# Feed-forward blocks of 512 tokens, one per batch, with the last 64 tokens of each batch set aside in DRAM for a ninth block

## The chip, the cores and the metric

The kernel runs on one core of one Trainium2 chip. The metric is the device time of one execution in microseconds. TensorE is called PE below (its weight loads PEld), VectorE DVE, ScalarE ACT, GpSimd POOL; SP is the engine that issues nearly all DMAs, from one queue in order.

## The reference

Eight batches of 576 tokens, model width 512. Each batch goes through attention over pooled keys and values, a two-dimensional Fourier transform whose real part is added, a normalization, and a feed-forward layer of width 2048, which holds most of the arithmetic:

```python
k_p = k.reshape(B, H, Sp, pool, D).mean(axis=3)          # pool = 8, Sp = 72
attn = softmax(scale * q @ k_p^T)                        # 8 heads of 64
x = (attn @ v_p).transpose(0, 2, 1, 3).reshape(B, S, 512)
mixed = np.real(fft(fft(x, axis=1), axis=2))
u = x + mixed
un = (u - mean(u)) / sqrt(var(u) + 1e-6)
out = u + np.maximum(un @ w_ch1, 0.0) @ w_ch2            # 512 -> 2048 -> 512
```

## The kernel before

**Two kinds of work share PE.** `fe(b)` is the front end of batch b: everything up to the normalized tokens. `ffn(...)` is the feed-forward layer on a block of token columns. Both are generators: each `yield` ends a stage, and the loop at the bottom of `tile_kernel` emits one stage of `ffn`, then the stages of front ends that are due (`advance`). A scheduler then places every instruction on its engine's queue, a fixed order in which the engine runs them; it can pull a front end's instructions ahead of or behind feed-forward matmuls.

**Front end.** With PE's tiles in the order in which they run: scores `psS` (L345) for four pairs of heads, transposes `psT`, `psV`, `psR`, values `psX`, then the transform over channels `psA` and `psB` (L547, L575), the transform over tokens `psQ` and `psP` (L592), the mean `psM` (L638 to L643) and the variance `psVar`. From `psQ` on the front end writes the batch's slot. The steps between the last of them: DVE adds `psP` to `X` (L607, L608), DVE sums two tiles into `s` (L617), ACT and DVE split `s` into two parts (L619, L620), POOL forms the four tiles of `U` (L624, L625), PE takes the mean (`psM`), DVE subtracts it (L644), ACT casts the result to `unh` (L632), DVE and POOL form the rest `unl` (L633). `unh` and `unl` are what the feed-forward matmuls read. The reciprocal deviation `rb` comes after that and is needed only when a block ends.

**The slots.** `U`, `unh`, `unl` and `rb` are rings of 1152 columns, two slots of 576: batch b lies in slot (b+1) mod 2. A front end may write its slot (stage "U") when the feed-forward layer has read the batch two before it; `free[b]` is the position at which that is so.

**Feed-forward.** A block takes 16 steps f, one for each 128 of the width 2048. A step has 12 matmuls into `g` (L731: `w1h` with `unh`, `w1h` with `unl`, `w1low` with `unh`, each over four channel tiles), ACT's relu to `hh` (L735), DVE's remainder `hl` (L736), and 12 matmuls into the four accumulators `acc` (L715). A step's second half is issued after the next step's first half. At the end of a block DVE multiplies each accumulator by `rb` (L745), adds it to `U` (L746), and SP writes `out` (L748). The blocks before: batch 0 in two halves of 288 columns, each in two passes over 8 steps; batches 1 to 6 in three rings of 1152 columns, each in three blocks of 384 that pass over the border between two batches; batch 7 in two blocks of 288. That is 208 steps, 64 of them with 288 columns and 144 with 384.

**Weights.** They come in 64-bit floats; 34 pieces are converted by ACT and DVE, split by ACT and POOL into a high part that stays and a low part that goes to DRAM (L205). Each step loads its two low parts of 256 KB back (L214), one step or more ahead, into a ring of 7 buffers that the conversion uses too. 11 pieces are converted before the first block (`AHEAD`), the others at positions that `PACE` and `LEAD` set.

Of the kernel before, what the change touches and what calls it, by code (L numbers as in the profile page):

```python
# [21 lines left out]
HS = S // 2  # L22
# [56 lines left out]
def raw(ap):  # L79
# [4 lines left out]
def tile_kernel(ctx: ExitStack, tc: tile.TileContext, qt, kt, vm, vr, w1, w2, cad, cbd, mkd, out):  # L84
# [76 lines left out]
    def load_w(n):  # L161
        if n >= len(pieces):
            return
        i, f, c, w, place = pieces[n]
        src = (w1, w2)[i][:, f, c * P:(c + w) * P]
        if not wide:
            st = wk.tile([P, DM], F32, tag="w", bufs=7, name="wraw")[:, 0:w * P]
            nc.sync.dma_start(st, src)
            staged[n] = st
            return  # L170
        if place is not None:
            st = wk.tile([P, 2 * DM], I32, tag=f"tail{place}", name="wst")
        else:
            st = wk.tile([P, DM], I32, tag="w", bufs=7, name="wraw")
        nc.sync.dma_start(st, src.bitcast(I32))
        staged[n] = st.rearrange("p (c m w) -> p c m w", m=P, w=2)

    def prep_w(n):
        if n >= len(pieces):
            return  # L180
        i, f, c, w, _ = pieces[n]
        cl = slice(c * P, (c + w) * P)
        if wide:
            st = staged.pop(n)
# [62 lines left out]
    def fe(b):  # L247
# [82 lines left out]
        def scores(gi, i):  # L330
# [371 lines left out]

    at = [0]

    def ffn(ro, nb, to, f0, f1):
        cl = slice(ro, ro + nb)
        acc = [pp.tile([P, 512], F32, tag=f"acc{e}", name=f"acc{to}_{f0}_{e}")[:, 0:nb] for e in range(4)]

        def gemm2(f, hh, hl, wh, wl):
            order = [(x, e) for x in range(3) for e in range(4)]  # L710
            if f == f1 - 1:
                order = [(x, e) for e in range(4) for x in range(3)]
            for x, e in order:
                w, h = ((wh, hh), (wl, hh), (wh, hl))[x]
                nc.tensor.matmul(acc[e], lhsT=w[:, e], rhs=h, start=(f == f0 and x == 0), stop=(f == f1 - 1 and x == 2))  # L715

        prev = None
        for f in range(f0, f1):
            step = at[0]
            at[0] += 1  # L720
            for m in range(2):
# [5 lines left out]
            ps = pp.tile([P, 512], F32, tag="g1", bufs=2, name=f"g1_{to}_{f}")[:, 0:nb]  # L727
            n = 0
            for w, x in ((ah, unh), (ah, unl), (al, unh)):
                for c, ti in enumerate((E0, O0, E1, O1)):  # L730
                    nc.tensor.matmul(ps, lhsT=w[:, c], rhs=x[:, ti, cl], start=(n == 0), stop=(n == 11))  # L731
# [7 lines left out]
                gemm2(f - 1, *prev)  # L739
                yield  # L740
            prev = (hh, hl, bh, bl)
        gemm2(f1 - 1, *prev)
        for e in range(4):
            u = U[:, e, cl]
            nc.vector.tensor_tensor(out=acc[e], in0=acc[e], in1=rb[:, cl], op=ALU.mult)  # L745
            nc.vector.tensor_tensor(out=u, in0=u, in1=acc[e], op=ALU.add)  # L746
            if f1 == NFC and e % 2:
                nc.sync.dma_start(out[:, e - 1:e + 1, to:to + nb], U[:, e - 1:e + 1, cl])  # L748
# [39 lines left out]
    def advance(pos):  # L790
        for b in sorted(run):
# [6 lines left out]
            while r[1] < upto:  # L798
# [133 lines left out]
```

## Time and profile before

| | before |
|---|---|
| median of 3 runs | 1094.45 us (1093.58 to 1095.3) |
| profiled execution: span | 1094.2 us |
| PE busy, share of the span | 1050.1 us, 96% |
| DVE, ACT, POOL busy | 611.6, 416.0, 247.3 us |
| DMA moved, mean rate | 175.80 MB, 161 GB/s |
| loads of low weights | 2 x 208 of 256 KB |
| PE instructions | 6606 |

The profiled execution is the span of 1094.2 us, 0.25 us from the median. In a timeline row stand the start, the busy time, the engine, the line, the operation, the tiles and their shape, the number of instructions merged into the row, and in brackets how long the engine had been idle before it and who released it. In a row of waits stand the total, the number and the longest. A row of groups has the busy time and the mean of one instruction.

### The profile page before, as it was taken

The numbers are of one execution on the slowest core, as the hardware profiler recorded it, in microseconds if no ns is written. First come the engines' busy times: TensorE is split into PE (matmuls) and PEld (weight loads), VectorE is DVE, ScalarE is ACT, GpSimd is POOL, SyncE is SP. The second block draws the span as 40 slices with busy tenths as digits, with TensorE's granted clock in tenths as the row PEclk, the third lists the DMA queues.
The fourth block names the chain that finished last, engine by engine and source line by source line (L and its number), as shares of the span: only waits on it lengthen the run. The fifth ranks groups of instructions, "written<-read, shape, count | busy, mean of one in ns | idle before, by whom it ended". The sixth has DMA issues, their size and how long they took to land.

```text
span 1094.2 us, 17702 instructions
## 1 busy us (share of the span) xinstructions
PE 1050.1 (96%) x6606; PEld 1017.7 (93%) x6606; DVE 611.6 (56%) x1237; ACT 416.0 (38%) x1102; POOL 247.3 (23%) x249
## 2 busy tenths in 40 slices
PE   8848898999999999999999999999999999999997
PEld 7637887999999999999999999999999999999997
DVE  7686878856376455756377455756467434522222
ACT  6767764443143331443233341443324322311110
POOL 4463356212230032201240121400322101200000
PEclk9968999999999999999999999999999999999999
DMA  7867977565345454445444444445534334346563
GB/s 242 274 204 254 318 250 227 178 199 170 119 122 161 121 162 135 127 140 166 131 120 148 142 151 130 133 125 156 158 108 155 98 98 124 117 128 189 165 186 99
DMA packets 91878, 175.80 MB, mean 161 GB/s; under 512 B 10128, under 2 KB 17296, under 8 KB 91536
## 3 DMA queue, kind: packets, MB, share of 16 engines
q1 hardware_dynamic: 91504, 172.01, 50.7%
q0 software_dynamic: 288, 2.66, 0.7%
q8 instruction: 52, 0.85, 0.3%
q14 instruction: 34, 0.28, 0.1%
HBM read 156.81 MB, written 17.83 MB: 160 GB/s over the span
## 4 chain that ended last, share of the span: by engine, by line
PE 84%; DVE 6%; DMA 4%; ACT 3%; issue 1%; POOL 1%; SPq 0%; DVEq 0%; POOLq 0%; ACTq 0%
PE acc L715 35%; PE g L731 35%; PE psX L432 3%; PE psS L345 3%; PE psA L547 2%; PE psP L592 2%; DMA wst<-in_w 1%; DMA w1low<-w1l 1%; PE psB L575 1%; PE psT L385 1%; DVE wd L199 1%; PE psQ L592 1%; DVE wd L198 1%; DMA k<-in_kt 1%; PE psR L408 1%
## 5 line engine op out<-in xcount | busy, mean ns | idle before, releaser
L735 ACT ACTIVATE hh<-g 128x384 fp32r<-128x384 f32 (+1 forms) x208 | 96.3, 464 | 309.6 <-PE g L731 289.8
L736 DVE SCALAR_TENSOR_TENSOR hl<-g,hh 128x384 fp32r<-128x384 f32 (+1 forms) x208 | 108.6, 522 | 185.0 <-ACT hh L735 183.2
L715 PE MATMUL acc<-hh,w2h 128*128 128x384 f32 (+1 forms) x832 | 190.9, 329 | 0.1
L715 PE MATMUL acc<-hh,w2low 128*128 128x384 f32 (+1 forms) x832 | 187.6, 328 | 1.2 <-DMA w2low<-w2l 1.2
L715 PE MATMUL acc<-hl,w2h 128*128 128x384 f32 (+1 forms) x832 | 182.6, 328 | 0.7 <-DVE hl L736 0.7
L731 PE MATMUL g<-unh,w1low 128*128 128x384 f32 (+1 forms) x832 | 178.7, 329 | 4.5 <-DMA w1low<-w1l 4.4
L731 PE MATMUL g<-unl,w1h 128*128 128x384 f32 (+1 forms) x832 | 178.1, 329 | 0.9 <-DVE unl L633 0.9
L731 PE MATMUL g<-unh,w1h 128*128 128x384 f32 (+1 forms) x832 | 175.4, 327 | 0.1
L731 PEld LDWEIGHTS g<-unh,w1low 128*128 128x128 f32 x832 | 140.8, 190 | 6.2 <-DMA w1low<-w1l 5.8
L715 PEld LDWEIGHTS acc<-hh,w2low 128*128 128x128 f32 x832 | 144.4, 189 | 2.0 <-DMA w2low<-w2l 1.4
L715 PEld LDWEIGHTS acc<-hh,w2h 128*128 128x128 f32 x832 | 143.2, 189 | 2.8 <-ACT rt L372 0.8
L715 PEld LDWEIGHTS acc<-hl,w2h 128*128 128x128 f32 x832 | 141.5, 190 | 1.5 <-DVE hl L736 0.9
L731 PEld LDWEIGHTS g<-unl,w1h 128*128 128x128 f32 x832 | 140.4, 190 | 2.1 <-DVE unl L633 1.3
L731 PEld LDWEIGHTS g<-unh,w1h 128*128 128x128 f32 x832 | 140.4, 190 | 1.5 <-issue 0.8
L364 POOL TENSOR_TENSOR t<-t,sm 128x720 f32<-128x720 f32 x32 | 45.9, 1434 | 286.7 <-DVE sm L363 248.0
L280 POOL TENSOR_TENSOR k<-k 128x288 f32<-128x288 f32 (+1 forms) x56 | 41.0, 732 | 97.6 <-DMA k<-in_kt 84.3
L624 POOL TENSOR_TENSOR U<-X,U 128x576 f32<-128x576 f32 (+1 forms) x14 | 20.0, 1433 | 129.2 <-DVE X L608 129.2
L349 DVE TENSOR_REDUCE mx<-psS 128x6 f32<-128x432 f32 (+1 forms) x64 | 33.1, 526 | 19.6 <-PE psS L345 19.3
L345 PE MATMUL psS<-kpb,q 128*128 128x144 f32 x280 | 42.7, 286 | 1.3 <-ACT w2h L203 0.9
L345 PEld LDWEIGHTS psS<-kpb,q 128*128 128x128 f32 x280 | 39.4, 189 | 1.7 <-ACT w2h L203 1.1
L360 ACT ACTIVATE t<-t 128x720 f32<-128x720 f32 x30 | 24.1, 804 | 37.1 <-DVE t L358 36.8
L745 DVE TENSOR_TENSOR acc<-acc,rb 128x384 f32<-128x384 f32 (+1 forms) x60 | 29.0, 517 | 13.5 <-PE acc L715 13.5
(209 smaller groups left out, 1426.9 us busy)
## 6 DMA issues: line engine op xcount, KB each, us to landing
w1low<-w1l SPq DMA_DIRECT2D x208, 256.0 KB, 2.8
w2low<-w2l SPq DMA_DIRECT2D x208, 256.0 KB, 2.9
wst<-in_w SPq DMA_DIRECT2D x30, 512.0 KB, 4.7
q<-in_qt SPq DMA_DIRECT2D x28, 288.0 KB, 3.1
k<-in_kt SPq DMA_DIRECT2D x28, 288.0 KB, 2.9
v<-in_vm SPq DMA_DIRECT2D x28, 256.0 KB, 3.0
out<-U SPq DMA_DIRECT2D x18, 384.0 KB, 3.6
w1l<-wd SPq DMA_DIRECT2D x16, 256.0 KB, 5.1
```

What stands on the lines that cost most here:

```text
L280: nc.gpsimd.tensor_tensor(out=out if n == 1 else src[:, :, 0:n], in0=src[:, :, 0] if n == 1 else src[:, :, 0:n], in1=src[:, :, 1] if n == ...
L345: mm = nc.tensor.matmul(ps[:, c * W2J:(c + 1) * W2J], lhsT=q[:, r0:r0 + P], rhs=kpb[g % 2], start=True, stop=True)
L349: nc.vector.tensor_reduce(out=mx[:, c0:c0 + n], in_=pv, op=ALU.max, axis=AX.X, negate=(b, g) in SM)
L360: nc.scalar.activation(t, t, AF.Exp, scale=1.0 / 64.0)
L364: ins = nc.gpsimd.tensor_tensor(out=t, in0=t, in1=sm.unsqueeze(3).broadcast_to([P, 5, 2, J]), op=ALU.mult)
L432: last = nc.tensor.matmul(ps, lhsT=w, rhs=a, start=(i == 0), stop=(i == len(mm) - 1))
L592: nc.tensor.matmul(ps, lhsT=w, rhs=a, start=(i == 0), stop=(i == 6))
L715: nc.tensor.matmul(acc[e], lhsT=w[:, e], rhs=h, start=(f == f0 and x == 0), stop=(f == f1 - 1 and x == 2))
L731: nc.tensor.matmul(ps, lhsT=w[:, c], rhs=x[:, ti, cl], start=(n == 0), stop=(n == 11))
L735: nc.scalar.activation(hh, ps, AF.Relu)
L736: nc.vector.scalar_tensor_tensor(out=hl, in0=ps, scalar=0.0, in1=raw(hh), op0=ALU.max, op1=ALU.subtract)
L745: nc.vector.tensor_tensor(out=acc[e], in0=acc[e], in1=rb[:, cl], op=ALU.mult)
```

## The change

`blocks()` now gives nine blocks of 512 columns: the first 512 tokens of each batch, in the slot where the batch lies, then a ninth block that is read from slot 0's place. All 16 steps run over each block: 144 steps. The first step of all is done in two column ranges, 288 and 224.

New are `keep_rest(b)`, issued when the front end of batch b has ended, which writes the last 64 columns of `unh`, `unl`, `U` and `rb` to four DRAM tiles `rests` (three DMAs of 128 KB and one of 32 KB for each batch, in pieces of 256 bytes), and `load_rest`, which before the ninth block reads the 8 x 64 columns of all batches back (three DMAs of 1 MB and one of 256 KB). The free positions, the pace of the weight conversion and the order in which the output is put together follow. `hh` and `hl` have 512 columns, and the ring of weight buffers has 6 places.

Lines of the changed kernel are 2 on from L731 (L733), L735 (L737) and L745 (L747); L715 keeps its number, as do those of the front end.

```diff
-AHEAD, LEAD, PACE = 11, 12, 0.65
+NB = 512
+RM = S - NB
+AHEAD, LEAD, PACE = 11, 8, 1.0
 def blocks():
-    r = [(slot(0) + h * HS, HS, h * HS, f, f + 8) for f in (0, 8) for h in range(2)]
-    for m in range(3):
-        r += [(i * 384, 384, S + m * RING + i * 384, 0, NFC) for i in range(3)]
-    return r + [(slot(7) + h * HS, HS, 7 * S + h * HS, 0, NFC) for h in range(2)]
+    return [(slot(b % B), b * NB) for b in range(B + 1)]
...
+    rests = [dp.tile([P, n, B, RM], F32, name=f"rest{i}") for i, n in enumerate((4, 4, 4, 1))]
...
-        lows[i, n] = t = wk.tile([P, DM], F32R, tag="w", bufs=7, name=f"w{i + 1}low")
+        lows[i, n] = t = wk.tile([P, DM], F32R, tag="w", bufs=6, name=f"w{i + 1}low")
...
-    def ffn(ro, nb, to, f0, f1):
-        cl = slice(ro, ro + nb)
+    def ffn(ro, to):
+        cl = slice(ro, ro + NB)
...
-            for w, x in ((ah, unh), (ah, unl), (al, unh)):
-                for c, ti in enumerate((E0, O0, E1, O1)):
-                    nc.tensor.matmul(ps, lhsT=w[:, c], rhs=x[:, ti, cl], start=(n == 0), stop=(n == 11))
-                    n += 1
-            hh = wk.tile([P, 384], F32R, tag="hh", bufs=2, name="hh")[:, 0:nb]
-            hl = wk.tile([P, 384], F32R, tag="hl", bufs=2, name="hl")[:, 0:nb]
+            for c0, c1 in ((0, HS), (HS, NB)) if step == 0 else ((0, NB),):
+                n = 0
+                for w, x in ((ah, unh), (ah, unl), (al, unh)):
+                    for c, ti in enumerate((E0, O0, E1, O1)):
+                        nc.tensor.matmul(ps[:, c0:c1], lhsT=w[:, c], rhs=x[:, ti, ro + c0:ro + c1], start=(n == 0), stop=(n == 11))
+                        n += 1
+            hh = wk.tile([P, NB], F32R, tag="hh", bufs=2, name="hh")
+            hl = wk.tile([P, NB], F32R, tag="hl", bufs=2, name="hl")
...
+    def keep_rest(b):
+        cl = slice(slot(b) + NB, slot(b) + S)
+        for t, r in zip((raw(unh), raw(unl), U), rests):
+            nc.sync.dma_start(r[:, :, b], t[:, :, cl])
+        nc.sync.dma_start(rests[3][:, 0, b], rb[:, cl])
+
+    def load_rest(ro):
+        cl = slice(ro, ro + NB)
+        for t, r in zip((raw(unh), raw(unl), U), rests):
+            nc.sync.dma_start(t[:, :, cl], r.rearrange("p n b s -> p n (b s)"))
+        nc.sync.dma_start(rb[:, cl], rests[3].rearrange("p n b s -> p (n b s)"))
-    free = {1: 0, 2: 64, 3: 128, 4: 160, 5: 224, 6: 256, 7: 320}
+    free = {b: 2 * NFC * (b - 1) for b in range(1, B)}
...
-        return max(AHEAD + PACE * pos, pos - 16 + LEAD)
+        return max(AHEAD + PACE * pos, pos + LEAD)
...
-    for blk in blocks():
+    for n, blk in enumerate(blocks()):
+        if n == B:
+            load_rest(blk[0])
```

How the queues of two engines change at a block's end: first PE, where the front end of batch 7 passes `psP`'s last matmuls in the queue before. The names give the tile and a running number (`psP_2_10037` is the last of three `psP`, `g_3648` the `g` of the block that starts at token 3648).

```order
L731 MATMUL g_3648_3_10110<-unh,w1low 128x384 x4
L592 MATMUL psP_2_10037<-cb,A_9128 128x290 x3
L592 MATMUL psP_2_10037<-cb,A_9129 128x290 x3
L592 MATMUL psP_2_10037<-cb,AB_9130 128x290
L715 MATMUL acc_0_0_9939<-hh,w2h 128x384
L715 MATMUL acc_0_1_9940<-hh,w2h 128x384
L715 MATMUL acc_0_2_9941<-hh,w2h 128x384
L715 MATMUL acc_0_3_9942<-hh,w2h 128x384
```

In the queue before, `psP` stands between two feed-forward steps, and `psM` follows it 36 feed-forward matmuls later. Now PE's queue at the same place of batch 5's front end, from `psP`'s last tile on; `g_2560` is the first tile of batch 5's own block.

```order
L592 MATMUL psP_2_5755<-cb,A_5388 128x290 x3
L592 MATMUL psP_2_5755<-cb,A_5389 128x290 x3
L592 MATMUL psP_2_5755<-cb,AB_5390 128x290
L345 MATMUL psS_3_0_5813<-kpb_80,q_3_5798 128x144 x3
L345 MATMUL psS_3_3_5819<-kpb_80,q_3_5798 128x144 x2
L642 MATMUL psM_5843<-s,avg 128x288
L643 MATMUL psM_5843<-s,avg 128x288
L642 MATMUL psM_5847<-s,avg 128x288
L643 MATMUL psM_5847<-s,avg 128x288
L345 MATMUL psS_2_0_5921<-kpb_79,q_2_5880 128x144 x3
L345 MATMUL psS_2_3_5927<-kpb_79,q_2_5880 128x144 x2
L733 MATMUL g_2560_0_6732<-unh,w1h 128x512
```

No feed-forward matmul stands between `psP` and `psM`, nor between `psM` and the first `g` of the block that needs the result. Ahead of these rows stand `psB`, `psQ` and the first two `psP`, again without a feed-forward matmul, and ahead of those the last matmuls of the block before. From `psP` on, the same stands at all seven places where a batch follows another (without the scores `psS` at the last). Second, DVE's queue before, where the end of a block meets batch 7's `psB`:

```order
L530 TENSOR_TENSOR B_9180<-psB_0_9182,B_9180 128x256
L745 TENSOR_TENSOR acc_0_0_9397<-acc_0_0_9397,rb 128x384
L530 TENSOR_TENSOR B_9181<-psB_1_9212,B_9181 128x256
L745 TENSOR_TENSOR acc_0_1_9398<-acc_0_1_9398,rb 128x384
L746 TENSOR_TENSOR U<-U,acc_0_0_9397 128x384
```

The two large `psB` parts are taken before most of the block's eight closing operations. Now the same on DVE, at the end of batch 4's block:

```order
L747 TENSOR_TENSOR acc_3_5660<-acc_3_5660,rb 128x512
L748 TENSOR_TENSOR U<-U,acc_0_5657 128x512
L748 TENSOR_TENSOR U<-U,acc_1_5658 128x512
L530 TENSOR_TENSOR B_5440<-psB_0_5442,B_5440 128x256
L748 TENSOR_TENSOR U<-U,acc_2_5659 128x512
L530 TENSOR_TENSOR B_5441<-psB_1_5472,B_5441 128x256
L748 TENSOR_TENSOR U<-U,acc_3_5660 128x512
L535 TENSOR_TENSOR AB_5390<-psB_2_5481,AB_5390 32x256
L598 TENSOR_TENSOR U<-X,psQ_1_5682 128x288
```

Three of the four multiplications stand ahead of these rows: all parts of `psB`, which `psQ` waits for, now follow six to eight of the closing operations.

More of the change, by code (lines that the diff above doesn't have):

```diff
@@ L166, in load_w @@
         if not wide:
-            st = wk.tile([P, DM], F32, tag="w", bufs=7, name="wraw")[:, 0:w * P]
+            st = wk.tile([P, DM], F32, tag="w", bufs=6, name="wraw")[:, 0:w * P]
             nc.sync.dma_start(st, src)
@@ L173, in load_w @@
         else:
-            st = wk.tile([P, DM], I32, tag="w", bufs=7, name="wraw")
+            st = wk.tile([P, DM], I32, tag="w", bufs=6, name="wraw")
         nc.sync.dma_start(st, src.bitcast(I32))
@@ L186, in prep_w @@
             halves = st.bitcast(U16)
-            d0 = wk.tile([P, DM], I32, tag="w", bufs=7, name="wd")[:, 0:w * P]
+            d0 = wk.tile([P, DM], I32, tag="w", bufs=6, name="wd")[:, 0:w * P]
             di = d0.rearrange("p (c m) -> p c m", m=P)
@@ L211, in load_low @@
     def load_low(i, n):
-        lows[i, n] = t = wk.tile([P, DM], F32R, tag="w", bufs=7, name=f"w{i + 1}low")
+        lows[i, n] = t = wk.tile([P, DM], F32R, tag="w", bufs=6, name=f"w{i + 1}low")
         nc.sync.dma_start(raw(t), wls[i][:, steps[n]])
-    steps = [f for *_, f0, f1 in blocks() for f in range(f0, f1)]
+    steps = [f for _ in blocks() for f in range(NFC)]
     turn, behind = [0], {}
@@ L368, in scores @@
                 if b == 0 and gi:
-                    st["rt", gi] = wk.tile([P, DM], F32, tag="w", bufs=7, name="rt0")[:, 0:10 * REM].rearrange("p (c r) -> p c r", c=5)
+                    st["rt", gi] = wk.tile([P, DM], F32, tag="w", bufs=6, name="rt0")[:, 0:10 * REM].rearrange("p (c r) -> p c r", c=5)
                 else:
@@ L703, in tile_kernel @@
     at = [0]
-    def ffn(ro, nb, to, f0, f1):
-        cl = slice(ro, ro + nb)
-        acc = [pp.tile([P, 512], F32, tag=f"acc{e}", name=f"acc{to}_{f0}_{e}")[:, 0:nb] for e in range(4)]
+    def ffn(ro, to):
+        cl = slice(ro, ro + NB)
+        acc = [pp.tile([P, NB], F32, tag=f"acc{e}", name=f"acc{to}_{e}") for e in range(4)]
         def gemm2(f, hh, hl, wh, wl):
             order = [(x, e) for x in range(3) for e in range(4)]
-            if f == f1 - 1:
+            if f == NFC - 1:
                 order = [(x, e) for e in range(4) for x in range(3)]
@@ L714, in gemm2 @@
                 w, h = ((wh, hh), (wl, hh), (wh, hl))[x]
-                nc.tensor.matmul(acc[e], lhsT=w[:, e], rhs=h, start=(f == f0 and x == 0), stop=(f == f1 - 1 and x == 2))
+                nc.tensor.matmul(acc[e], lhsT=w[:, e], rhs=h, start=(f == 0 and x == 0), stop=(f == NFC - 1 and x == 2))
         prev = None
-        for f in range(f0, f1):
+        for f in range(NFC):
             step = at[0]
@@ L726, in ffn @@
             ah, al, bh, bl = [x.rearrange("p (c m) -> p c m", m=P) for x in (high(0, f), lows[0, step], high(1, f), lows[1, step])]
-            ps = pp.tile([P, 512], F32, tag="g1", bufs=2, name=f"g1_{to}_{f}")[:, 0:nb]
-            n = 0
-            for w, x in ((ah, unh), (ah, unl), (al, unh)):
-                for c, ti in enumerate((E0, O0, E1, O1)):
-                    nc.tensor.matmul(ps, lhsT=w[:, c], rhs=x[:, ti, cl], start=(n == 0), stop=(n == 11))
-                    n += 1
-            hh = wk.tile([P, 384], F32R, tag="hh", bufs=2, name="hh")[:, 0:nb]
-            hl = wk.tile([P, 384], F32R, tag="hl", bufs=2, name="hl")[:, 0:nb]
+            ps = pp.tile([P, NB], F32, tag="g1", bufs=2, name=f"g1_{to}_{f}")
+            for c0, c1 in ((0, HS), (HS, NB)) if step == 0 else ((0, NB),):
[6 more added lines that the diff above has]
+            hl = wk.tile([P, NB], F32R, tag="hl", bufs=2, name="hl")
             nc.scalar.activation(hh, ps, AF.Relu)
@@ L741, in ffn @@
             prev = (hh, hl, bh, bl)
-        gemm2(f1 - 1, *prev)
+        gemm2(NFC - 1, *prev)
         for e in range(4):
@@ L746, in ffn @@
             nc.vector.tensor_tensor(out=u, in0=u, in1=acc[e], op=ALU.add)
-            if f1 == NFC and e % 2:
-                nc.sync.dma_start(out[:, e - 1:e + 1, to:to + nb], U[:, e - 1:e + 1, cl])
+            if e % 2:
+                nc.sync.dma_start(out[:, e - 1:e + 1, to:to + NB], U[:, e - 1:e + 1, cl])
         yield
-    free = {1: 0, 2: 64, 3: 128, 4: 160, 5: 224, 6: 256, 7: 320}
+    def keep_rest(b):
[9 more added lines that the diff above has]
+    free = {b: 2 * NFC * (b - 1) for b in range(1, B)}
     npre = 20
@@ L777, in tile_kernel @@
                 pass
+            keep_rest(0)
         if n >= NEXT and n2 < 8:
@@ L780, in tile_kernel @@
             n2 += 1
+    keep_rest(1)
     while n2 < STEPS:
@@ L808, in advance @@
                     del run[b]
+                    keep_rest(b)
                     break
     def need(pos):
-        return max(AHEAD + PACE * pos, pos - 16 + LEAD)
+        return max(AHEAD + PACE * pos, pos + LEAD)
     pos = 0
-    for blk in blocks():
+    for n, blk in enumerate(blocks()):
+        if n == B:
+            load_rest(blk[0])
         for _ in ffn(*blk):
@@ L927 @@
     o = r.results[0]["out_0"]
-    o = o.transpose(2, 1, 0).reshape(B, S, DM)
+    o = o.transpose(2, 1, 0).reshape(B * S, DM)
+    o = np.concatenate([o[:B * NB].reshape(B, NB, DM), o[B * NB:].reshape(B, RM, DM)], 1)
     got = np.empty((B, S, DM), np.float32)
```

## The prediction

> **What bounds the kernel now.** I read the page first: the engines' busy time, and the span in 40 slices of 27.4 us.
>
> ```profile
> PE 1050.1 (96%) x6606; PEld 1017.7 (93%) x6606; DVE 611.6 (56%) x1237; ACT 416.0 (38%) x1102; POOL 247.3 (23%) x249
> PE   8848898999999999999999999999999999999997
> PEclk9968999999999999999999999999999999999999
> GB/s 242 274 204 254 318 250 227 178 199 170 119 122 161 121 162 135 127 140 166 131 120 148 142 151 130 133 125 156 158 108 155 98 98 124 117 128 189 165 186 99
> ```
>
> From the ninth slice on PE never rests, while DVE is at 56%. So PE's own work sets the time, and what counts is how much of it there is and whether PE must ever wait. The waits of PE from 60 us to the end come next.
>
> ```profile
> PE psT L385 <- POOL t L364: 7.3, 1, 7.3
> PE psM L638 <- DVE s L617: 6.0, 1, 6.0
> PE g L731 <- DMA w1low<-w1l: 4.4, 4, 1.9
> PE psVar L698 <- DVE X L695: 3.4, 1, 3.4
> PE psR L408 <- ACT ah L390: 1.7, 1, 1.7
> PE acc L715 <- DMA w2low<-w2l: 1.2, 1, 1.2
> ```
>
> The two largest, 13.3 us, lie before the first feed-forward matmul: there batch 0's front end has nothing to run beside it, and PE waits for its chain. No other front end costs PE such a wait, because feed-forward matmuls fill the gaps. Then the stretches with feed-forward matmuls alone (six steps of 384 columns, then 288), and the start and end of the feed-forward part in the timeline.
>
> ```profile
> core 0: us, PE busy (x) PEld busy (x) DVE busy (x) ACT busy (x) POOL busy (x), PEclk, DMA share, GB/s
> 60.00:90.00 30.00, 15.75 (x79) 14.26 (x80) 24.93 (x46) 20.70 (x62) 17.27 (x13) 0.66 0.64 206
> 956.63:981.84 25.21, 25.21 (x145) 25.21 (x145) 7.12 (x12) 4.32 (x8) 0.00 (x0) 1.00 0.43 125
> 1040.00:1085.00 45.00, 45.00 (x341) 45.00 (x340) 7.32 (x17) 5.78 (x15) 0.00 (x0) 1.00 0.53 159
> ```
> ```profile
> 76.94 2.03 PE L731 MATMUL g<-unh,w1h 128*128 128x288 f32 x7
> ...
> 1087.41 0.69 PE L715 MATMUL acc<-hl,w2h 128*128 128x288 f32 x4
> 1090.05 1.12 SPq L748 DMA_DIRECT2D out<-U  x2
> ```
>
> **Part 1, wider matmuls.** Six steps are 144 matmuls: 25.21 / 144 = 175.1 ns for 384 columns; 45.00 / 341 = 132.0 ns for 288. The difference is 0.449 ns a column, so 512 columns should take 175.1 + 128 x 0.449 = 232.5 ns. Before: 3456 x 175.1 + 1536 x 132.0 = 807.9 us. After: 144 x 24 = 3456 x 232.5 = 803.5 us. All of it lies on PE's path: **-4.4 us**. If 512 columns cost in proportion to 384 (233.5 ns), it is -1; I let it go to -8.
>
> **Part 2, the first block.** A new low weight is needed every 24 x 232.5 = 5.6 us instead of every 3.2, but all 16 pairs are now needed within 89 us, not 102. The waits for `w1low` and `w2low` above, 5.6 us together, shrink but need not vanish: **-4 us** (0 to -6). The waits for `psVar` and `psR` stay.
>
> **Part 3, the boundary.** This is the term that decides. PE's queue now holds a bare front end at each of seven places: from the block's last matmul through `psB`, `psQ`, `psP`, `psM` to the next block's first `g`. What that chain takes I read where batch 7's front end passes it, in the timeline of all engines.
>
> ```profile
> 930.04 0.29 PE L592 MATMUL psP<-cb,AB 98*128 98x290 f32 x1
> 930.17 0.86 PE L715 MATMUL acc<-hh,w2h 128*128 128x384 f32 x4
> 930.43 0.74 DVE L607 TENSOR_TENSOR X<-X,psP 128x574 f32<-128x574 f32 x1
> 931.28 0.76 DVE L617 TENSOR_TENSOR s<-X 128x576 f32<-128x576 f32 x1
> 933.41 1.82 POOL L625 TENSOR_TENSOR U<-X,U 128x576 f32<-128x576 f32 x1
> 937.27 0.43 PE L643 MATMUL psM<-s,avg 128*128 128x288 f32 x2
> 937.67 2.62 DVE L644 TENSOR_TENSOR X<-U,psM 128x1152 f32<-128x1152 f32 x2 [1.96 <-PE psM L643]
> 940.33 2.40 ACT L632 CAST unh<-X 128x576 fp32r<-128x576 f32 x4 [0.46 <-DVE X L644]
> 942.23 2.92 POOL L633 TENSOR_TENSOR unl<-X,unh 128x576 fp32r<-128x576 f32 x2 [7.00 <-ACT unh L632]
> ```
>
> Each waits for those above it. From `psP`'s end (930.17) to the end of the first cast (940.33 + 2.40 / 4 = 940.93) are 10.8 us. In it `psM` was held behind feed-forward matmuls: L644 needs POOL's `U`, ready at 935.23, and began at 937.67, 2.4 us late. So 8.4 us remain. In their place DVE has the next batch's scores to do, from these groups:
>
> ```profile
> L361 DVE TENSOR_REDUCE sm<-t 128x10 f32<-128x720 f32 x30 | 27.0, 899 | 15.3 <-ACT t L360 15.0
> L349 DVE TENSOR_REDUCE mx<-psS 128x6 f32<-128x432 f32 x32 | 19.3, 603 | 17.0 <-PE psS L345 16.8
> L358 DVE TENSOR_TENSOR t<-psS,mx 128x432 f32<-128x432 f32 x30 | 18.0, 600 | 1.2 <-DVE mx L349 0.5
> L745 DVE TENSOR_TENSOR acc<-acc,rb 128x384 f32<-128x384 f32 x36 | 19.3, 557 | 11.6 <-PE acc L715 11.6
> L745 DVE TENSOR_TENSOR acc<-acc,rb 128x288 f32<-128x288 f32 x24 | 9.8, 457 | 1.9 <-PE acc L715 1.9
> ```
>
> Some 3 us, of which the wait for POOL hides most; I take 9.6 us. PE has of its own in that time two sets of scores and `psM`: in the rows below six `psS` pass in 0.64 us, so ten in 1.1; `psM` has 0.5 us (four matmuls of 288 columns). That leaves 9.6 - 2.7 = 6.9 us of waiting.
>
> ```profile
> 806.86 0.90 PE L345 MATMUL psS<-kpb,q 128*128 128x144 f32 x6
> 807.50 0.78 PE L715 MATMUL acc<-hl,w2h 128*128 128x384 f32 x3
> 913.92 0.86 PE L575 MATMUL psB<-ca,f 128*32 128x256 f32 x6
> ```
>
> Ahead of `psP`: L745 takes 557 ns for 384 columns and 457 for 288, so 690 for 512, and its add about as much. Eight of them are 5.5 us, and `psB`'s last part, which `psQ` needs, comes after them: `psQ` ends its first tile some 5.5 us after the block's last matmul, while PE has 18 `psB` and 6 `psQ` to do, 2.8 us at about 0.12 (132.0 less 32 x 0.449 ns for 256 columns). That is 2.7 us of waiting, and 0.5 more where `psP` waits for banks that DVE has still to empty. Behind the first cast, the casts and `unl` end 4.2 us later (942.23 + 2.92 = 945.15), while the 16 matmuls that can run are 3.7: 1 us with the order of POOL's queue. Sum: 6.9 + 3.2 + 1.0 = 11.1 us a boundary.
>
> The clock comes on top. In the window from 60 to 90 us, around the one bare front end of the kernel before, PE's clock was 0.66. Half of a boundary's own matmuls and the first steps after it would run slower; I add 2.4 us. **13.5 us each, 94.5 us in all.** Bounds: 7 us (the chain behind `psP` with no more) and 18 (the 13.3 us that PE waited at batch 0, and 5 of clock).
>
> The Trainium skill, "TensorE: Matmul & The Clock Gate", section "Why this matters for your kernels", advises to leave no gap over some 3 us between bursts of matmuls, since one idle window halves the clock. This trace agrees, with its 0.66. By that page's window of 3.4 us, an estimate of the least cost is 1.7 us a boundary, 12 us in all, where I have 17.
>
> **Part 4, the rest.** `keep_rest`'s stores and `load_rest`'s loads stand on SP's queue, where a waiting DMA holds up the low weights behind it. The loads come at the start of batch 7's block, after its stores, each waiting for its store to land.
>
> ```profile
> w1low<-w1l SPq DMA_DIRECT2D x208, 256.0 KB, 2.8
> w1l<-wd SPq DMA_DIRECT2D x16, 256.0 KB, 5.1
> w2l<-wd SPq DMA_DIRECT2D x4, 128.0 KB, 3.4
> ```
>
> Two such stores of 128 KB are 6.8 us, and 2 MB of loads at the 318 GB/s that the page's busiest slice shows are 6.6 us, ahead of the fourth step's low weights, which are needed three steps (16.7 us) after the block's start. Cover and load are close: **+2 us** (0 to 5). At the six other batches the stores are only issued, and six ring places hold three steps: nothing. The last closing operations have 512 columns, not 288: **+1 us**.
>
> The Trainium skill, "DMA: Bandwidth & Descriptors", section "Specifications", says that pieces under 512 bytes make the DMA read, modify and write; the stores have pieces of 256. No run here shows it yet. If they took as long as 256 KB, each store would be 1.7 us later, and the term 5 instead of 2.
>
> **Sum** against the profiled execution: 1094.2 - 4.4 - 4 + 94.5 + 2 + 1 = **1183 us**; the median of the runs differs from its span by 0.25 us.
>
> **The rivals.** *Order stalls inside the block too.* A front end's way from its first scores (806.86) to its last `psB` (913.92) took 107.1 us beside feed-forward matmuls. A block after the change holds 16 x 5.58 = 89.3 us of them. Front ends have 1088.1 - 76.9 - 807.9 - 10.7 (the waits listed after 77 us) = 192.6 us of PE now, 27.5 for each of seven, of which 9.4 fall to the boundary; so the block lasts 89.3 + 18 = 107 us: equal. For it: the scheduler gave the front end all of the block, so there is no slack. Against it: the nines of PE's row, where such waits would show today. If the chain is 5 us longer than the block, six times: 1183 + 30 = 1213 us. 12%.
>
> *The chain hides.* PE has 53 matmuls of `psB`, `psQ`, `psP`, about 6.7 us, and 2.7 of scores and mean at each boundary. If the chain from the last feed-forward matmul to the first cast took no more than 10 us, PE would hardly wait, and parts 1 and 2 would win: 1094.2 - 8.4 + 3 = 1089 us. For it: DVE has no `hl` to do meanwhile. Against: the half behind `psP` alone has 8.4 us at least. 5%.
>
> *The ring is too small.* With six places shared by conversion and low weights, each of the first 16 steps might wait 1.1 us, as the four waits for `w1low` did (4.4 / 4): 1183 + 18 = 1201 us. Against: a step is now 1.7 times as long. 5%.
>
> **How the numbers follow.** The forecast has 76%; its own range is 1094.2 - 14 + 49 + 1 = 1130 to 1094.2 - 1 + 126 + 6 = 1225. The two slower rivals lie inside it, so I cut it to 1130 to 1220. About 0.2% is what a measurement of this kernel can tell from no change. Faster 0.05 (the chain hides), the same 0.02 (it nearly does), slower 0.93.
>
> **What would show it.** Right: PE's row of slices has seven dips, 110 to 130 us apart; the waits list `psM` behind DVE's `s` and `g` behind ACT's `unh`, six or seven times each; feed-forward matmuls 232 ns apart. Wrong: a PE row without dips, or waits spread over the blocks (`psX`, `psT`, `w1low`). If the waits at boundaries sum to under 10 us, part 3 fails.

## The result, and the profile after

The changed kernel takes 1176.84 us (median of 4 runs, 1175.23 to 1178.1), the kernel before 1094.88 us on the same chip: ratio 1.0748, 95% interval 1.0731 to 1.0765. The profiled execution has a span of 1176.3 us.

The page of the changed kernel first: busy times, PE's row and its clock in slices of 29.4 us, and the DMA packets.

```profile
PE 1074.3 (91%) x5082; PEld 870.4 (74%) x5082; DVE 606.5 (52%) x1125; ACT 408.5 (35%) x1038; POOL 247.3 (21%) x249
PE   7859889699989999899979997999989996999997
PEclk9979989899998999899989999999989998999999
DMA packets 86806, 148.83 MB, mean 127 GB/s; under 512 B 21840, under 2 KB 22352, under 8 KB 86480
```

PE was at 96% and rested nowhere after the ninth slice; now its row has a dip every four to five slices, and the clock dips with it. In the trace these are seven stretches without a feed-forward matmul: 17.7, 17.9, 22.5, 21.7, 21.7, 21.7 and 18.5 us long (141.7 in all), 122 to 127 us apart. What PE waits for from 230 us on (total, number, longest), which holds the last six of them:

```profile
PE psS L345 <- DVE X L644: 11.7, 5, 2.5
PE psB L575 <- DVE B L530: 8.8, 4, 2.4
PE psM L643 <- DVE s L620: 6.8, 6, 1.4
PE psM L642 <- DVE t L358: 6.6, 4, 1.7
PE g L733 <- ACT unh L632: 6.5, 2, 5.1
PE psM L642 <- ACT s L619: 4.8, 2, 2.5
PE psP L592 <- DVE U L599: 1.8, 1, 1.8
PE psQ L592 <- DVE AB L535: 1.6, 4, 1.2
PE psQ L592 <- DVE B L530: 0.8, 1, 0.8
PE psS L345 <- DVE X L608: 0.5, 3, 0.2
```

All are tiles of the bare front end or its first consumer. None is a weight, and none lies inside a block. The sum is 49.9 us, 8.3 for each of the six. One of these boundaries in the timeline of all engines, from the block's last matmuls to the next block's first:

```profile
587.58 1.07 PE L715 MATMUL acc<-hl,w2h 128*128 128x512 f32 x4
588.00 2.49 DVE L747 TENSOR_TENSOR acc<-acc,rb 128x512 f32<-128x512 f32 x4 [1.85 <-PE acc L715]
591.73 0.42 DVE L530 TENSOR_TENSOR B<-psB,B 128x256 fp32r<-128x256 f32 x1
592.20 0.89 PE L575 MATMUL psB<-ca,f 128*32 128x256 f32 x6 [2.14 <-DVE B L530]
598.65 0.29 PE L592 MATMUL psP<-cb,AB 98*128 98x290 f32 x1
598.76 3.28 POOL L624 TENSOR_TENSOR U<-X,U 128x576 f32<-128x576 f32 x2 [14.58 <-DVE X L608]
602.00 3.28 POOL L625 TENSOR_TENSOR U<-X,U 128x576 f32<-128x576 f32 x2
602.10 1.91 DVE L620 TENSOR_TENSOR s<-s 128x576 fp32r<-128x576 f32 x1
604.06 0.40 PE L643 MATMUL psM<-s,avg 128*128 128x288 f32 x1 [1.37 <-DVE s L620]
605.31 0.90 DVE L361 TENSOR_REDUCE sm<-t 128x10 f32<-128x720 f32 x1 [0.93 <-ACT t L360]
606.13 2.61 DVE L644 TENSOR_TENSOR X<-U,psM 128x1152 f32<-128x1152 f32 x2
607.53 2.77 PE L345 MATMUL psS<-kpb,q 128*128 128x144 f32 x10 [2.50 <-DVE X L644]
608.77 2.39 ACT L632 CAST unh<-X 128x576 fp32r<-128x576 f32 x4 [3.49 <-DVE X L644]
609.92 2.83 PE L733 MATMUL g<-unh,w1h 128*128 128x512 f32 x7
```

The chain can be read down the rows: `psB`'s last tile waits for its bank behind DVE's closing operations; POOL's four sums end at 605.28; L644 needs them, and begins 0.85 us later, behind a sum for the next batch's scores (L361) in DVE's queue; the casts need L644; `g` needs the first cast. Then the clock (the number after POOL's) around the boundary:

```profile
601.00:605.00 4.00, 1.25 (x4) 0.67 (x4) 3.38 (x5) 1.07 (x2) 4.00 (x3) 1.00 0.27 74
605.00:609.00 4.00, 1.50 (x7) 1.48 (x7) 3.66 (x5) 0.51 (x2) 0.28 (x1) 0.52 0.16 39
609.00:613.00 4.00, 4.00 (x15) 3.45 (x14) 3.70 (x5) 3.41 (x8) 3.73 (x3) 0.63 0.36 92
```

The spacing of matmuls is read from start to start, in stretches with feed-forward matmuls alone: over six steps of 512 columns in the changed kernel, and over eleven of 288 in the kernel before (24 matmuls each).

```profile
1003.78 1.10 PE L733 MATMUL g<-unh,w1h 128*128 128x512 f32 x4
1037.18 1.10 PE L733 MATMUL g<-unh,w1h 128*128 128x512 f32 x4
```
```profile
1044.93 0.70 PE L731 MATMUL g<-unh,w1h 128*128 128x288 f32 x4
1080.04 0.69 PE L731 MATMUL g<-unh,w1h 128*128 128x288 f32 x4
```

That is 33.40 us / 144 = 231.9 ns and 35.11 / 264 = 133.0 ns. Dividing a window by the number of its instructions, as the prediction did for 288 columns (132.0) and the expectations below do for 512 (229.8), comes out about 1% low, since matmuls that stick out over the window's ends are counted whole. Where the 82.1 us between the two spans lie, counted on PE's trace (each matmul from its start to the next one's start or its own end, whichever is first; the remainder is idle):

| PE, us | before | after | difference |
|---|---|---|---|
| feed-forward matmuls | 829.2 | 827.4 | -1.8 |
| of this, number x own spacing | 809.4 | 801.4 | -8.0 |
| of this, above it (slow clock, turns with the front end) | 19.8 | 26.0 | +6.2 |
| other matmuls | 220.9 | 246.9 | +26.0 |
| idle | 36.2 | 91.8 | +55.6 |
| ahead of the first and behind the last matmul | 7.9 | 10.2 | +2.3 |

### The profile page after: what moved, and what is told of

It is laid out like the page before. It is cut to its first block, busy times and chain, and to the rows that moved or that the text cites. A ratio compares the mean times of both kernels' runs of the same rounds, so it can differ in the third digit from the quotient of the medians.

```text
span 1176.3 us, 14209 instructions
## 1 busy us (share of the span) xinstructions
PE 1074.3 (91%) x5082; PEld 870.4 (74%) x5082; DVE 606.5 (52%) x1125; ACT 408.5 (35%) x1038; POOL 247.3 (21%) x249
## 2 busy tenths in 40 slices
DMA packets 86806, 148.83 MB, mean 127 GB/s; under 512 B 21840, under 2 KB 22352, under 8 KB 86480
## 4 chain that ended last, share of the span: by engine, by line
PE 73%; DVE 11%; DMA 5%; POOL 4%; issue 4%; ACT 3%; SPq 0%; POOLq 0%; DVEq 0%; ACTq 0%
PE acc L715 31%; PE g L733 30%; PE psX L432 3%; PE psS L345 2%; DVE X L644 2%; DMA wst<-in_w 2%; POOL unl L633 2%; PE psP L592 1%; PE psA L547 1%; DVE acc L747 1%; DMA w1l<-wd 1%; PE psT L385 1%; PE psQ L592 1%; DVE U L748 1%; PE psB L575 1%
## 5 line engine op out<-in xcount | busy, mean ns | idle before, releaser
L738 DVE SCALAR_TENSOR_TENSOR hl<-g,hh 128x512 fp32r<-128x512 f32 x144 | 98.9, 688 | 279.9 <-ACT hh L737 278.9
L737 ACT ACTIVATE hh<-g 128x512 fp32r<-128x512 f32 x144 | 85.8, 596 | 292.2 <-PE g L733 286.1
L715 PE MATMUL acc<-hh,w2h 128*128 128x512 f32 x576 | 174.6, 403 | 3.5 <-ACT hh L737 3.3
L733 PE MATMUL g<-unh,w1h 128*128 128x512 f32 (+2 forms) x580 | 169.5, 413 | 6.5 <-ACT unh L632 6.5
L733 PE MATMUL g<-unl,w1h 128*128 128x512 f32 (+2 forms) x580 | 167.1, 399 | 2.6 <-DVE unl L633 2.2
L715 PE MATMUL acc<-hh,w2low 128*128 128x512 f32 x576 | 166.6, 396 | 0.0
L733 PE MATMUL g<-unh,w1low 128*128 128x512 f32 (+1 forms) x580 | 161.1, 395 | 0.3 <-DMA w1low<-w1l 0.3
L715 PE MATMUL acc<-hl,w2h 128*128 128x512 f32 x576 | 161.1, 395 | 0.0
L733 PEld LDWEIGHTS g<-unh,w1h 128*128 128x128 f32 x580 | 114.2, 200 | 33.5 <-ACT unh L632 7.3
L733 PEld LDWEIGHTS g<-unl,w1h 128*128 128x128 f32 x580 | 107.1, 189 | 29.8 <-DVE unl L633 4.6
L715 PEld LDWEIGHTS acc<-hh,w2h 128*128 128x128 f32 x576 | 106.0, 189 | 28.7 <-ACT hh L737 5.0
L733 PEld LDWEIGHTS g<-unh,w1low 128*128 128x128 f32 x580 | 108.0, 188 | 25.6 <-DMA w1low<-w1l 0.6
L715 PEld LDWEIGHTS acc<-hl,w2h 128*128 128x128 f32 x576 | 107.2, 188 | 23.9 <-issue 0.4
L715 PEld LDWEIGHTS acc<-hh,w2low 128*128 128x128 f32 x576 | 107.7, 189 | 23.0 <-issue 0.8
L624 POOL TENSOR_TENSOR U<-X,U 128x576 f32<-128x576 f32 (+1 forms) x14 | 20.2, 1464 | 131.6 <-DVE X L608 106.5
L349 DVE TENSOR_REDUCE mx<-psS 128x6 f32<-128x432 f32 (+1 forms) x64 | 32.1, 523 | 15.3 <-PE psS L345 15.2
L747 DVE TENSOR_TENSOR acc<-acc,rb 128x512 f32<-128x512 f32 x36 | 23.3, 692 | 21.4 <-PE acc L715 21.4
```

The lines of the kernel that those rows point to most:

```text
L349: nc.vector.tensor_reduce(out=mx[:, c0:c0 + n], in_=pv, op=ALU.max, axis=AX.X, negate=(b, g) in SM)
L715: nc.tensor.matmul(acc[e], lhsT=w[:, e], rhs=h, start=(f == 0 and x == 0), stop=(f == NFC - 1 and x == 2))
L733: nc.tensor.matmul(ps[:, c0:c1], lhsT=w[:, c], rhs=x[:, ti, ro + c0:ro + c1], start=(n == 0), stop=(n == 11))
```

## The experiments

Each ratio is to the kernel before, run beside it on the same chip. A difference in us to the changed kernel goes across chips, on which the kernel before took 1093.84 to 1095.58 us, so 2 us of it mean nothing.

**More work in each block.** The dummies lie in `ffn`, ahead of a step's first matmul:

```diff
+                for _ in range(3 if to < 7 * NB and step else 0):
+                    nc.tensor.matmul(ps, lhsT=ah[:, 0], rhs=unh[:, 0, cl], start=True, stop=True)
```

> The changed kernel with three more matmuls of 512 columns in each step of the first seven blocks, 333 in all, into the tile that the step's own first matmul overwrites: 333 x 229.8 ns = 76.5 us more for PE, 11 us for each block. Theory A (the order: a bare front-end chain of some 20 us stands at each boundary and has a length of its own): the time rises by the whole 76.5 us, to 1253, and the bare stretches between blocks stay 18 to 22 us long. Theory B (the pace-maker: one front end takes some 126 us from the scores to the casts, the next one cannot begin earlier, and a boundary is what is left of the 126 us when the block's matmuls are used up): the 11 us of each block take the place of waiting and of slow clock; the period between boundaries stays 125 to 129 us, the stretches shrink, and the time is 1175 to 1200.

Measured: 1242.58 us, 65.7 over the changed kernel; ratio 1.1357 (1.1334 to 1.138). Of the 77 us added (333 x 231.9 ns), only 11 were taken up. On the time theory A was nearly right and theory B wrong: from one front end's first scores to the next one's, the period grew from 126 to some 138 us. On the other sign theory A failed: the seven stretches without a feed-forward matmul are 12.0 to 17.7 us long, 15.2 on average, where the changed kernel has 20.2.

**Without DRAM.** `keep_rest` and `load_rest` are not called.

> The changed kernel without the two steps by way of DRAM: nothing is set aside and nothing is read back, so the ninth block works on whatever its slot holds and the 64 last tokens of each batch are not computed. Theory A and theory B both: the stores and loads are hidden, 1173 to 1178 us. Rival (the 256-byte pieces and SP's queue cost 1.7 us or more a batch and some us ahead of the ninth block): 1155 to 1165 us.

Measured: 1184.53 us, ratio 1.0832 (1.0816 to 1.0848): 7.7 us slower than with them, outside both ranges. 5.3 us of this are there by 350 us, in a starting phase for which the scheduler gave another order. From the first scores of batch 3's front end (351.7 us here, 346.4 in the changed kernel) to the end the two traces take 830.6 and 829.9 us, so behind the start the stores and loads cost nothing that their absence would give back. The DMA rows of the changed kernel (KB each, median us to landing), with stores of the same size in larger pieces last:

```profile
rest<-U SPq DMA_DIRECT2D x8, 128.0 KB, 2.4
rest<-unh SPq DMA_DIRECT2D x8, 128.0 KB, 2.7
rest<-unl SPq DMA_DIRECT2D x8, 128.0 KB, 2.2
w2l<-wd SPq DMA_DIRECT2D x4, 128.0 KB, 2.7
```

**Whole batches in narrow blocks,** made from the kernel before:

```diff
-    for m in range(3):
-        r += [(i * 384, 384, S + m * RING + i * 384, 0, NFC) for i in range(3)]
-    return r + [(slot(7) + h * HS, HS, 7 * S + h * HS, 0, NFC) for h in range(2)]
+    return r + [(slot(b) + h * HS, HS, b * S + h * HS, 0, NFC) for b in range(1, B) for h in range(2)]
...
-    free = {1: 0, 2: 64, 3: 128, 4: 160, 5: 224, 6: 256, 7: 320}
+    free = {b: 64 * (b - 1) for b in range(1, B)}
```

> The kernel before with batches 1 to 6 in two blocks of 288 columns each, as batches 0 and 7 are already, so that all 576 tokens of a batch lie between two boundaries and no block passes over the border between batches. PE's feed-forward work by the spacings is 6144 x 132.0 = 811 us instead of 807.9. Theory A (a block that ends where a batch ends puts the next front end bare on PE): six or seven boundaries at 8 to 13 us, 1145 to 1190 us. Theory B: a batch now gives 101 us of feed-forward and some 27 of front-end matmuls, more than the chain's 126, so nothing is bare and the time is 1094 to 1110 us.

Measured: 1103.48 us, ratio 1.0089 (1.0073 to 1.0105). From 230 us on PE waited 0.5 us in all. A block that ends with its batch is thus not enough to lay a front end bare: theory A falls.

**A shorter front end:**

```diff
             prep_k(1)
-            yield from scores(1, 1)
+            st["t", 1] = st["t", 0]
+            nc.scalar.copy(out=st["rt", 1][:, :, REM:2 * REM], in_=st["t", 1][:, :, P:W2J])
+            yield
```

> The changed kernel without the scores and the softmax of the fourth pair of heads in batches 2 to 7 (the third pair's result is used again): ten matmuls of 144 columns, 1.3 us of PE, go from each of six front ends, but some 18 us go from its chain. Theory A: only the matmuls' time goes, and the bare stretches, which lie behind this place, stay: 1166 to 1172 us. Theory B: the chain is shorter by what the pair took, so each boundary comes 10 to 18 us earlier and little of it stays bare: 1070 to 1120 us.

Measured: 1168.59 us, ratio 1.069 (1.067 to 1.071): 8.2 us less, 1.4 for each front end, about what its matmuls alone are worth. From the first scores to the last `psB` a front end took 112.0 us (mean of the last five) where the changed kernel takes 119.6: 7.6 us less, not 18. And these were lost again behind `psB`, where new waits stand (1.8 us in the changed kernel):

```profile
PE psP L594 <- DVE U L601: 9.2, 7, 2.0
PE psP L594 <- DVE U L610: 4.5, 5, 2.0
```

`psP` comes earlier against the block's end now and meets DVE's closing operations. Theory B falls here a second time.

In the changed kernel the last `psB` passes behind the block's last matmul. At the last five boundaries of this run it passes some 5 us ahead of it (708.86 and 713.90 us at one of them), and in the run with more work 7 to 8 us, with no wait of PE between the two. Yet the second half of `psQ` stands among or behind the block's last matmuls in PE's queue, and all of `psP` behind them. A lead of this size goes unused by PE's order; why the scheduler set it so is open.

So the first theory explains the first and the fourth run and fails in the third, the second one the reverse. The rows of PE's first `psS` and last `psB` of one front end show what both had left out. First the changed kernel (steps of 24 x 231.9 ns = 5.6 us), then the run with more work (27 x 231.9 ns = 6.3 us a step), then the run with blocks of 288 columns (3.2 us):

```profile
598.82 0.97 PE L345 MATMUL psS<-kpb,q 128*128 128x144 f32 x6
718.61 0.89 PE L575 MATMUL psB<-ca,f 128*32 128x256 f32 x6 [2.35 <-DVE B L530]
```
```profile
633.06 0.97 PE L345 MATMUL psS<-kpb,q 128*128 128x144 f32 x6
755.40 0.86 PE L575 MATMUL psB<-ca,f 128*32 128x256 f32 x6
```
```profile
774.58 0.90 PE L343 MATMUL psS<-kpb,q 128*128 128x144 f32 x6
873.21 0.87 PE L573 MATMUL psB<-ca,f 128*32 128x256 f32 x6
```

That is 119.8, 122.3 and 98.6 us, and 107.1 in the rows that the prediction shows of the kernel before, with steps of 4.2 us. The last five front ends to the last of these matmuls have means of 119.6, 123.9, 100.3 and 109.8 us (the expectation below counts to the first `psB`, 5 to 7 us less). The front end's way gets longer as the steps beside it do. Theory C: the stages take their turns among the feed-forward work, so a wide step stretches the front end, and the block of 512 tokens at the same time offers less to cover it. The next run has the same tokens, DRAM path and first and last block as the changed kernel, and halves the steps, which gives twice as many of them:

```diff
-    return [(slot(b % B), b * NB) for b in range(B + 1)]
+    r = [(slot(0), 0, NB)]
+    r += [(slot(b) + h * NB // 2, b * NB + h * NB // 2, NB // 2) for b in range(1, B) for h in range(2)]
+    return r + [(slot(0), B * NB, NB)]
...
-    def ffn(ro, to):
+    def ffn(ro, to, nb):
...
-    free = {b: 2 * NFC * (b - 1) for b in range(1, B)}
+    free = {b: 2 * NFC * max(b - 1, 2 * b - 3) for b in range(1, B)}
```

> The changed kernel with the blocks of batches 1 to 7 cut into two of 256 columns; batch 0 and the ninth block keep 512, and the 64 last tokens still go by way of DRAM. A batch gives PE about as much as before the cut (768 matmuls at an estimated 118 ns by the spacings of 288 and 384 columns, 90 us, against 384 x 229.8 ns = 88 us), but a step lasts 2.8 us instead of 5.5. Theory A (a bare chain at each boundary, whatever the block): 1177 + 14 = 1191 us. Theory B (a pace-maker of 126 us a batch): the same period, 1170 to 1190 us. Theory C, formed from the first four runs (from the scores to psB a front end took 95 us beside steps of 3.2 us, 104 beside 4.2, 115 beside 5.5 and 117 beside 6.2: each of its stages waits for its turn among the feed-forward work, so wide steps stretch it): with short steps a front end takes some 92 us to psB, is done before its block begins, no boundary is bare, and the time is 1085 to 1110 us.

Measured: 1116.11 us, ratio 1.0193 (1.0172 to 1.0214): 60.7 us faster than the changed kernel, though its matmuls should take longer. PE's row of its page, its waits from 230 us on, the starts of two steps of 256 columns that lie seven steps apart, and one front end:

```profile
PE   8849897889999999999999999999999999999996
```
```profile
PE psA L549 <- DVE f L506: 2.1, 1, 2.1
PE acc L717 <- DVE hl L740: 0.8, 1, 0.8
PE acc L717 <- DVE U L750: 0.2, 1, 0.2
```
```profile
949.55 0.63 PE L735 MATMUL g<-unh,w1h 128*128 128x256 f32 x4
969.41 0.64 PE L735 MATMUL g<-unh,w1h 128*128 128x256 f32 x4
```
```profile
654.29 0.90 PE L347 MATMUL psS<-kpb,q 128*128 128x144 f32 x6
750.55 0.86 PE L577 MATMUL psB<-ca,f 128*32 128x256 f32 x6
```

The six dips behind the first are gone, the waits fell from 49.9 to 3.1 us, and the front end's way is 96.3 us beside steps of 24 x 118.2 ns = 2.8 us (19.86 us / 168 = 118.2 ns). The narrower matmuls cost 5376 x 118.2 ns - 2688 x 231.9 ns = 12.1 us, so the six bare boundaries were worth 60.7 + 12.1 = 72.8 us, 12.1 each. Theories A and B gave 1170 us or more. The time is above theory C's range by 6 us. The feed-forward matmuls took 25 us above their spacings here, against 20 in the kernel before, and PE was idle for 42.6 us against 36.2; why is open.

Half the step also means twice as many steps, and so twice as many places where the loop puts in a stage of the front end. Wider and fewer are told apart only by the run with more work: there the number of steps is that of the changed kernel, a step is 0.7 us longer, and the front end 4.3 us. So the width has a part in it; the number was not tried alone.

**Dummies in the waits.** The lines stand in `ffn`'s first step; the front end keeps the last `psS` and `psM` matmul in `behind`:

```diff
+            for k, m, n in (("S1", 1, 6), ("M1", 0, 10)) if f == 0 and 1 < to // NB < B - 1 else ():
+                with tc.issue_after(behind[k, to // NB + m].ins):
+                    for _ in range(n):
+                        nc.tensor.matmul(ps[:, 0:P], lhsT=ident, rhs=ident, start=True, stop=True)
```

> The changed kernel with 16 matmuls of 128 columns of the identity in PE's waits at five of the seven boundaries (6 behind the next batch's first scores, 10 behind psM), written to the tile that the next block's first matmul overwrites. They last no longer than the waits they stand in. The prediction's own 2.4 us of slow clock a boundary: 5 x 2.4 us at best, 1165 to 1177 us. If the slow clock is the larger part (the trace has 12 us on feed-forward and 23 us on front-end matmuls, 5 us a boundary): 1150 to 1162 us. If the dummies only delay what is queued behind them: 1177 to 1185 us.

Measured: 1189.25 us, ratio 1.0864 (1.0834 to 1.0894), 12.4 us slower: at the boundary near 600 us, ten of them behind `psM` lasted 3.9 us in a wait of 2.5, and delayed the scores and `g`. With 4 and 5 dummies instead:

> As the first run with dummy matmuls in the waits of five boundaries, but with 4 and 5 of them instead of 6 and 10, which lay on the path there (ten behind psM lasted 3.9 us in a wait of 2.5). If a higher clock behind the wait is worth anything: 1155 to 1172 us. If the dummies bring no clock worth having: 1175 to 1186 us.

Measured: 1181.63 us, ratio 1.0786 (1.0769 to 1.0802), still 4.8 us slower. The dummies did raise the clock: in 16 us around the boundary near 600 us its mean is 0.89 in both versions (603 to 619, 600 to 616 us), where the changed kernel has 0.79 (598 to 614 us). Whatever that was worth, the dummies cost more; what the slow clock alone costs stays an estimate from the trace.

**DVE's closing operations later** (the front end keeps `psP`'s last addition in `behind`):

```diff
+            late = behind.get(("P", to // NB + 1))
+            with tc.issue_after(late.ins) if late else ExitStack():
-            nc.vector.tensor_tensor(out=acc[e], in0=acc[e], in1=rb[:, cl], op=ALU.mult)
+                nc.vector.tensor_tensor(out=acc[e], in0=acc[e], in1=rb[:, cl], op=ALU.mult)
```

> The changed kernel with DVE's closing operations of a block (four products, and the sums that need them) held behind the last addition of psP of the next front end, so that psB's parts and psQ's differences no longer wait behind them. By the prediction's 3.2 us a boundary ahead of psP: 1177 - 7 x 3.2 = 1155 us at best, 1155 to 1168. If DVE then is late for s, the scores and the mean behind psP: 1172 to 1182 us.

Measured: 1178.64 us, ratio 1.0765 (1.0745 to 1.0785): 1.8 us over the changed kernel, next to no change. Its waits show where the gain went:

```profile
PE psM L642 <- DVE t L358: 31.1, 5, 6.2
```

`psB`'s 8.8 us of waiting have shrunk to 0.8, but `psM` waits 31.1 us at five boundaries behind DVE's `t`, which was 6.6 at four. The closing operations only moved behind `psP`.

**POOL's sums shared with DVE** (`UE = [4, 1, 2]` instead of `[4, 1, 0]`):

> The changed kernel with two of the four sums that form U done by DVE instead of POOL in batches 2 to 7. POOL's four take 6.5 us behind the last psP; two take 3.3 us. If POOL's sums are what holds the mean's subtraction: up to 3.2 us at each of six boundaries, 1157 to 1168 us. If DVE's own queue (s, its split, the next batch's scores) is as long: 1172 to 1180 us.

Measured: 1184.41 us, ratio 1.0819 (1.0788 to 1.0851), 7.6 us slower, so worse than either expectation. Here too the wait of `psM` behind DVE's `t` grew, to 17.7 us at five boundaries. DVE has little room behind `psP`: it is busy for 14.4 of the 16 us from 598 us on in the changed kernel, and for 15.1 in this run.

**The ring alone** (`bufs=6` for `bufs=7` in the kernel before):

> The kernel before with one edit, the ring of weight buffers at 6 places instead of 7. The prediction's rival (the ring is too small) has 1.1 us a step in the first 16 steps of the changed kernel; in the kernel before, with steps of 3.2 to 4.2 us, it would be worse: 1105 us or more. If the ring is no limit: 1092 to 1098 us.

Measured: 1094.24 us against 1095.58, ratio 0.9985 (0.9975 to 0.9994). Six places are no limit in the kernel before.

**Where a wide block starts to cost.** Two versions of the run with 256 columns, with batches 6 and 7, or 4 to 7, at 512 again:

```diff
+WIDE = {0, 6, 7, 8}
...
+    r = []
+    for b in range(B + 1):
+        n = 1 if b in WIDE else 2
+        r += [(slot(b % B) + h * NB // n, b * NB + h * NB // n, NB // n) for h in range(n)]
+    return r
```

> The run with blocks of 256 columns, but with batches 6 and 7 in blocks of 512 again (1 to 5 stay at 256). Theory C: a front end beside short steps gains on the blocks, so that by batch 6 it is a good part of a block ahead; one wide block uses up some 20 us of that and no boundary is bare: 1116 less 2 x 1.6 us of matmuls, 1108 to 1117 us. Theory A (whatever precedes it, a block of 512 columns ends in a bare front end): 13 us more for the boundary behind batch 6's block, 1122 to 1130 us.

Measured: 1109.64 us, ratio 1.0126 (1.011 to 1.0143). No boundary is bare.

> As the run before, but with batches 4 to 7 in blocks of 512 columns. Theory C: the lead that the front ends have won by batch 4 is used up by the first wide block and a part of the second, so the boundaries ahead of batches 6 and 7 are bare and the one ahead of batch 5 hardly: 1116 - 6 + 2 x 11 to 13 us, 1125 to 1140 us. Theory A: three bare boundaries, 1145 to 1152 us. If wide blocks late in the program cost nothing: 1105 to 1115 us.

Measured: 1139.6 us, ratio 1.0401 (1.0375 to 1.0427): 30.0 us more, for two more wide batches. PE's row, in slices of 28.5 us:

```profile
PE   7859888799999999999999998999799997999997
```

Behind the start it is whole up to a light dip in the slice from 684 us, ahead of batch 5, and has full dips in the slices from 798 and 940 us, ahead of batches 6 and 7. The first wide block lives on the lead that the front ends had won, the next ones do not: theory C's sequence. No version here beats the kernel before. That its 384 columns are the best between both costs is likely, not shown: the kernel before also differs in its blocks and has no way by DRAM.

## Why the prediction was right, and where its steps failed

Predicted 1183 us (1130 to 1220), measured 1176.84: the likeliest case came, by its mechanism. Of its signs, the seven dips (122 to 127 us apart), `psM` behind DVE's `s` (six times) and feed-forward matmuls 232 ns apart came; `g` behind ACT's `unh` is listed twice, not six or seven times. That the number came within 7 us is in part luck: the seven boundaries were some 9 us cheaper than forecast (7 x 12.2 = 85 us) and the matmuls 4, while all the rest came out 6 us dearer (82.1 + 8.0 - 85.4 = 4.7, where -4 + 2 + 1 = -1 was forecast). Step by step:

**Part 1, wider matmuls: -4.4, measured -8.0.** This term was mis-sized, and lies at its own bound. The wide matmuls came at 231.9 ns where the slope between 288 and 384 columns had given 232.5 (-2.1 us); those of 288 columns take 133.0 ns, not 132.0, so the kernel before spent 1.5 us more on them than the prediction reckoned. 256 columns take 118.2 ns. Little of the gain was left: feed-forward matmuls as a whole take 1.8 us less, since 6.2 us more lie above the spacing.

**Part 2, weights in the first block: -4.** The waits for `w1low` and `w2low` (5.6 us) shrank to 0.3. Whether that gave time is not shown, for other waits took their place: PE is idle for 41.7 us by 230 us, with one bare boundary in it, against 36.2.

**Part 3, the boundaries: 13.5 us each, measured some 12.** The six boundaries from 230 us on are 20.7 us long on average. Less the 9.4 us that the prediction gave to PE's own matmuls, 11.3 are lost, and 6.2 / 7 = 0.9 more on feed-forward matmuls: 12.2. The run with 256 columns gives 12.1 by its own way. Inside, the split was off: waits are 8.3 us, not 11.1. Behind `psP` the rows of `psM`, of `psS` behind `X` L644 and of `g` sum to 36.4 / 6 = 6.1 us, where 7.9 were given; ahead of `psP` 13.0 / 6 = 2.2, where 3.2 were given. The remainder of the 12.2, 3.9 us, is more than the 2.4 put down to the clock. Around these six boundaries the granted clock is 0.50 for 51.2 us in all, in 34.4 of which PE is busy; if work takes twice as long then, an estimate is 17.2 us, 2.9 a boundary at most. What is left, 1 us, is not told apart.

At the boundary shown the clock was 0.50 from 605.14 to 611.97 us, behind a stretch in which PE was busy 1.25 of 4 us, though no wait there is over 2.5 us. The Trainium skill, "TensorE: Matmul & The Clock Gate", section "Why this matters for your kernels", warns of gaps over some 3 us. Here several shorter ones in a row came ahead of it. The least cost of 1.7 us a boundary that the prediction worked out from that page lies below the 2.9.

**Part 4, the rest by way of DRAM: +2, measured nothing to give back.** The stores of 128 KB landed in 2.2 to 2.7 us, not 3.4, and from 230 us on PE waited for no low weight. The Trainium skill, "DMA: Bandwidth & Descriptors", section "Specifications", has pieces under 512 bytes read, modified and written. The changed kernel moves 21840 packets under 512 bytes, the kernel before 10128; the stores in such pieces landed no later than stores of 128 KB in larger ones (2.7 us), so no cost shows at this size, and the 5 us that I had worked out beside it did not come.

**The rivals.** *The chain hides* failed: 49.9 us of waits. *The ring is too small* failed: waits for `w1low` are 0.3 us in all, and six places cost nothing in the kernel before either. *Order stalls inside the block* rested on a front end of 107.1 us. That number was read beside steps of 4.2 us and used for steps of 5.6. The front end became 119.8 us long, more than the 5 us over the block that the rival asked for; yet no wait appeared inside a block, and the 30 us did not come on top. Block and boundary are one sum: a longer front end shows as a boundary that stays bare, which part 3 had priced already.

**The cause.** The prediction read PE's order and said that the front end stands bare; it did not say why it can't stand elsewhere. The runs showed the condition: with half the step, the same tokens and the same path by DRAM, six boundaries vanish, and with wide blocks put back at the end they return from the second one on. In the changed kernel a front end (119.6 us to its last `psB`) is not done within a block (126 - 20.7 = some 105 us). Three things stay open: why a wide step stretches a front end (which engine's queue a stage waits in), why leaving out a quarter of the scores shortened it by only 7.6 us, and why a lead of 5 to 8 us at a block's end is not used.

## What to carry to other kernels

When a block of the main work hides another chain, a change of the block can change both sides: here each front end had 512 tokens of feed-forward work beside it instead of 576, and that chain got longer beside wider steps (96 us beside 2.8, 120 beside 5.6). That each of its stages waits its turn among larger pieces is the likely reason, not a shown one. So read the chain's length beside steps of two or three sizes before using it for a fourth. And when a bare chain has several engines at the same length, moving work from one to another can just move the wait, and dummy work in a wait can lengthen the chain, as both did here.

## What the runs showed of the hardware

At full clock matmuls of 512 columns came every 231.9 ns and those of 256 every 118.2 ns, so doubling the width saved 4.5 ns in 236. The granted clock fell to 0.50 for 6.8 us at a boundary whose waits, one by one, were no longer than 2.5 us. DRAM stores in pieces of 256 bytes landed in 2.2 to 2.7 us for 128 KB.
